# A quad's q and k loaded by 128 places, its -1 rows sent behind them, gates' inputs later, a new table of rules

## The chip, the cores and the metric

The kernel runs on one core of a Trainium2 chip, in one launch. The metric is the time of that launch on the device in microseconds (us), and lower is better. All times below come from runs of the kernel before, and from one execution of it that was profiled.

## The reference, cut to what matters

Two attention layers, A and B, work on the same input x (2048 tokens of 640 numbers), each with weights of its own, and a gate for each token mixes their outputs. A layer has 32 heads of 20 numbers, and goes through the tokens in 4 segments of 512. In a segment each head does causal softmax attention, and reads a memory M, z that the segments before have filled:

```python
for s in range(N):                                   # N = 4 segments of L = 512
    qs, ks, vs = q[:, :, s], k[:, :, s], v[:, :, s]
    logits = einsum("bhqd,bhkd->bhqk", qs, ks) * scale + mask
    a_dot = einsum("bhqk,bhkd->bhqd", softmax(logits), vs)
    a_mem = (phi(qs) @ M) / (phi(qs) @ z + 1e-6)
    outs.append(g * a_mem + (1.0 - g) * a_dot)
    M, z = M + phi(ks).T @ vs, z + phi(ks).sum()     # by head
...
g = sigmoid((x * gate_w).sum(-1, keepdims=True))
return g * layer(x, A) + (1 - g) * layer(x, B)
```

## The kernel before, in words

**Windows and quads.** The work is cut into 8 windows t: 4 segments times 2 layers. A window first makes q, k and v by products with the weights. TensorE works in a reduced f32 form, so each factor is split into a high and a low part, and a product is three products (high by high, low by high, high by low). The q and k so made (three rows for each number: the high part, the low part, and one of the two again) are written to DRAM tiles `qd[t]` and `kd[t]` and read back in another arrangement: 8 *quads* u of 4 heads each, 64 quads i = 8t + u in all.

**A quad's tiles.** `qst` and `kst` (4 buffers of each, `NQ`) are tiles of 128 places (partitions) by 2 pairs by 512 tokens. Two heads stand above each other, at places 0 and 64, and the pairs stand side by side. A head takes 3 x 20 = 60 places. The next two places of a head hold, in q, the high and low part of each row's maximum, and in k the number -1, so that a product over 62 places gives a score less its row's maximum.

**Loading a quad** (`load_quads`, L1013). Four DMAs fill a quad's tiles: q and k, each for the upper and the lower half of the places. One such DMA moves 60 places of 2 pairs of 512 numbers; its source is walked as 60 x 2 x 512, and so is its destination. The -1 rows are written once, at the start, by a memset of each whole k tile on POOL (L276), and no load touches them. A quad can be loaded when its q and k are in DRAM and the quad that had the buffer 4 quads ago is done with it (`t_over`).

**A quad's steps.** S units (`s_unit`) make scores, and DVE finds their row maxima (L1058). The maxima are turned by TensorE and sent by two small DMAs into the q tile (L1108). T units (`t_unit`) then make the transposed scores with the maxima taken off, ACT takes the exponential (L1153), and POOL cuts it at the diagonal (L1154). `pv_unit` multiplies by v (L1181), and `fin_unit` weighs and stores the result.

**What sets the order.** The kernel writes its instructions out by hand, with a small planner: a clock of its own, a queue for each of ACT, DVE, POOL and SP with a cost for each instruction, and two lanes for the two halves of TensorE's rows. A product of 128 rows is cut in two halves of 64 rows, which run beside each other. For each of the slots i (`RULES`, L90) a row of the table gives the order of S and T units and five numbers: how far the units are spread over the slot, how loaded DVE may be for side work, the lag before a unit goes on in the other half, the room that is kept, and how early the slot begins. The planner only fixes the order in which each engine gets its instructions. On the chip each engine takes its own in that order and waits where data are not there. All DMAs are issued from SP's queue, in its order; an instruction that waits there holds up all behind it. Between slots TensorE is filled with the products for this window and the next (`fill_gen`).

**The gate.** `token_gate` loads 4 tiles of x and weighs them with `gate_w`; the first 4 are asked for at job 4.

**The end.** The last window's output product is split: `job_early` does 3 of 5 blocks k of the contraction, and `job_last` (L976) the other two, after the last transposes. Each block k needs the transposed output in two parts, high (ACT) and low (DVE, from the high part). For each of 5 row tiles m, `finish` adds what was kept and sends the sum to the output.

Of the kernel before, what the change touches and what calls it, by code (L numbers as in the profile page):

```python
# [18 lines left out]
P = 128  # L19
D = 640  # L20
# [17 lines left out]
def r32(ap):  # L38
    return ap.bitcast(F32)
# [3 lines left out]
def tile_gated_mix_infini_attn(  # L43
# [44 lines left out]


    RULES = {  # L90
        0: "STSTSTSTST 1.010 2.38 0.36 8 0.0",
        1: "TSTSTSTSTS 1.010 2.19 0.30 8 0.0",
        3: "TSTSTSTSTS 1.010 2.38 0.30 8 0.0",
        4: "TSTSTSTSTS 1.010 2.38 0.32 6 0.0",
        5: "TTSSTTSSTS 1.010 2.38 0.30 8 0.0",
        6: "TSTSTSTSTS 1.010 2.38 0.30 8 0.0",
        8: "TSTSTSTSTS 1.045 2.38 0.30 4 0.0",
        9: "TSTSTSTSTS 1.010 2.38 0.35 8 0.0",
        10: "TSTSTSTSTS 1.021 2.38 0.32 8 0.0",
        12: "TSTSTSTSTS 1.010 2.38 0.30 8 0.0",  # L100
        14: "TSTSTSTSTS 0.957 2.38 0.37 6 0.0",
        15: "TSTSTSTSTS 0.932 2.30 0.32 8 0.0",
        16: "TSTSTSTSTS 1.010 2.38 0.30 8 0.0",
        19: "TSTSTSTSTS 1.002 2.63 0.30 8 0.0",
        21: "TSTSTSTSTS 1.010 2.51 0.30 4 0.0",
        22: "TSTSTSTSTS 0.927 1.90 0.30 4 0.0",
        23: "TTSTSTSTSS 1.012 2.26 0.37 8 0.0",
        24: "TSTSTSTSTS 1.010 2.38 0.30 8 0.0",
        25: "TSTSTSTSTS 1.010 3.35 0.30 8 0.0",
        27: "TSTSTSTSTS 1.010 2.38 0.30 8 0.0",  # L110
        28: "TSTSTSTSTS 0.939 3.03 0.35 8 0.0",
        30: "TSTSTSTSTS 1.010 2.38 0.30 8 0.0",
        32: "TTSTSTSTSS 1.010 2.38 0.30 8 0.0",
        34: "TSTSTSTSTS 1.010 2.38 0.30 8 0.0",
        36: "TSTSTSTSTS 1.040 2.50 0.30 6 0.0",
        37: "TSTSTSTSTS 0.950 2.38 0.30 6 0.0",
        39: "TSSTTSSTTS 1.010 1.60 0.37 8 0.0",
        41: "TSSTTSSTTS 1.010 2.38 0.33 6 0.0",
        42: "TSTSTSTSTS 0.939 2.38 0.30 4 0.0",
        46: "TSTSTSTSTS 1.010 2.38 0.30 8 0.0",  # L120
        49: "TSTSTSTSTS 1.010 2.38 0.25 4 0.0",
        50: "TSTSTSTSTS 1.010 2.38 0.30 8 0.0",
        54: "TSSTTSSTTS 1.019 3.32 0.30 6 0.0",
        57: "TSTSTSTSTS 1.010 2.38 0.30 8 0.0",
        58: "TSTSTSTSTS 1.014 3.04 0.30 8 0.0",
        60: "TSTSTSTSTS 1.010 2.38 0.30 8 0.0",
        61: "STSTSTSTST 1.047 2.95 0.38 8 6.0",
        62: "TSTSTSTSTS 1.010 2.38 0.30 8 0.0",
        63: "TSTSTSTSTS 1.014 2.38 0.25 4 0.0",
        64: "TSTSTSTSTS 1.010 2.38 0.30 8 0.0",  # L130
    }
    rule = {}
    DONE = {"A": 0.165, "D": 0.11, "G": 0.1, "S": 0.0}
# [32 lines left out]
    def put(e, dur, emit, then=None, prio=5):  # L166
        heapq.heappush(ready[e], (prio, next(seq), dur, emit, then))
        load[e] += dur
        start_next(e)

    def dma(us, emit, then=None, prio=5, lat=1.1, some=False):

        def issued():
            dma_free[0] = max(clk[0] + 0.9, dma_free[0]) + us
            if not some:
                dma_free[0] = dma_free[1] = max(dma_free[0], clk[0] + 0.9 + us, dma_free[1] + us)
            if then:
                at(dma_free[0] + lat, then)

        put("S", 0.37, emit, issued, prio)  # L180
# [88 lines left out]
    def small_tiles():  # L269
        make_identity(nc, ident)  # L270
        nc.gpsimd.memset(tri, 0.0)
        nc.gpsimd.affine_select(
            out=tri[:, L - P:], in_=tri[:, L - P:], pattern=[[-1, P]], base=0,
            channel_multiplier=1, compare_op=ALU.is_ge, fill=NEG,
        )
        for t in kst:  # L276
            nc.gpsimd.memset(r32(t), -1.0)

    def idle_step():
        z = qst[0][:, 0, :]  # L280
# [293 lines left out]

    Ot = {}
    O_store = Store([sb.tile([P, NB, D], F32, tag=f"O{i}", name=f"O{i}", bufs=1) for i in range(2)])
    OTs = {}
    pqTs = {}
    arrived = set()
    qk_done = set()  # L580
# [395 lines left out]
    def job_last(t):  # L976

        s = t // 2
        pps = {}

        def finish(m):
            if m not in kept:
                at(clk[0] + 0.3, lambda: finish(m))
                return
            put("D", 0.63, lambda: nc.vector.tensor_tensor(  # L985
                out=r32(kept[m]), in0=pps[m], in1=r32(kept[m]), op=ALU.add), lambda: dma(
                    0.7, lambda: nc.sync.dma_start(
                        out=outT[P * m:P * (m + 1), L * s:L * (s + 1)], in_=r32(kept[m])), prio=2), prio=2)

        for k in range(SOON, KT):  # L990
            yield from hold_on(lambda: (t, k) in OTs, "last")
            oh, ol = OTs[t, k]
            for m in range(KT):
                wh, wl = split[job_index[t, "early", m]]
# [3 lines left out]
                for j, (w, o) in enumerate(((wh, oh), (wl, oh), (wh, ol))):  # L998
                    yield from hold_on(lambda: not any((*firsts, *seconds, *lane_ops)), "last")
                    whole(STEP, lambda: nc.tensor.matmul(  # L1000
                        pps[m], lhsT=w[:, k, :], rhs=o, start=(k == SOON and j == 0), stop=(k == KT - 1 and j == 2)))
                    yield STEP
                if k == KT - 1:
                    after_whole(lambda m=m: finish(m))


# [1 line left out]
        t, u = divmod(i, 8)  # L1008
        return t, u, qst[i % NQ], kst[i % NQ]

    loaded, next_load, t_over = set(), [0], set()

    def load_quads():  # L1013

        while next_load[0] < 64:
            i = next_load[0]
            t, u, q, k = quad(i)
            m = (80 * u + 79) // P
            if any((t, kind, mm) not in qk_done for kind in "qk" for mm in range(m + 1)):
                return  # L1020
            if i >= NQ and i - NQ not in t_over:
                return
            next_load[0] += 1
            done = then_all(4, lambda i=i: loaded.add(i))
            r0, soon = 80 * u, marks[i - LEAD] if i >= LEAD else -2
            for dst, src in ((q, qd[t]), (k, kd[t])):
                rows = src[r0:r0 + 80, :, :].rearrange("(p f d) c n -> f (d c) p n", p=2, f=2)
                for half in range(2):
                    dma(1.0, lambda dst=dst, src=rows[half], half=half: nc.sync.dma_start(
                        out=r32(dst[64 * half:64 * half + 3 * DH, :, :]), in_=r32(src)), done, prio=soon)  # L1030

    mx, m_done, mr_done = {}, set(), set()
    t_done, p_done, s_left = {}, {}, {}
# [232 lines left out]
    def o_transpose(t, k):  # L1266
        b = bank.free.pop(0)
        px = b.rearrange("p (n c) -> p n c", c=P)

        def got(hi, lo):  # L1270
            def end():
                bank.give(b)
                OTs[t, k] = (hi, lo)

            put("A", 0.49, lambda: nc.scalar.copy(hi, b), lambda: put("D", 0.63, lambda: nc.vector.tensor_tensor(
                out=lo, in0=b, in1=r32(hi), op=ALU.subtract), end, prio=2), prio=2)
# [164 lines left out]


    warm_up()
    put("G", 6.0, small_tiles, prio=0)
    put("G", 1.6, ones_tiles, prio=1)
    for k in range(KT):
        if k < len(HEAD0):
# [89 lines left out]
```

## Time and profile before

| What | us |
|---|---|
| Time, median of 3 runs (lowest, highest) | 1039.98 (1039.63, 1041.46) |
| The profiled execution's own time | 1040.3 |
| Its span, from the first to the last instruction | 1038.6 |
| ACT busy | 661.7 |
| POOL busy | 581.7 |

The granted clock of TensorE is 0.999 over the whole span. The span lies 1.7 us below the profiled execution's own time, which is the median of the runs shown to within 0.4 us, so numbers worked out from the trace can be set against either.

The profile's page gives the busy time of each engine, the time of the DMA packets, the chain of work that ended last, the costliest groups of instructions and the DMA issues. A window's row gives, for a stretch of the span, the busy time of PE, PEld, DVE, ACT and POOL, the granted clock, the share of the time that the 16 DMA engines were busy, and GB/s.

### The profile page before, as it was taken

What the parts mean: (1) busy time and instruction counts of PE and PEld (TensorE: products, weight loads), DVE (VectorE), ACT (ScalarE), POOL (GpSimd) and SP (SyncE); (2) the same over time, 40 slices, a digit from 0 to 9 for tenths busy, and PEclk for the clock granted to TensorE, in tenths of its full rate; (3) what the DMA queues carried; (4) which work ended last, traced back from release to release, by engine and by line L of the source; (5) the groups of instructions that cost most, each with busy time, mean ns of one, the idle gap of its engine ahead of it and who ended that gap; (6) DMA issues with size and microseconds to landing.
All of it is one profiled execution on the core that took longest, in us unless ns stands there. A gap on an engine that the chain in (4) does not pass through costs nothing.

```text
span 1038.6 us, 31967 instructions
## 1 busy us (share of the span) xinstructions
PE 1031.3 (99%) x11780; PEld 874.8 (84%) x11780; DVE 765.4 (74%) x2726; ACT 661.7 (64%) x1336; POOL 581.7 (56%) x1043
## 2 busy tenths in 40 slices
PE   9999999999999999999999999999999999999998
PEld 7988888898888879898888978989879888888876
DVE  4687787579686788676886868865787867778764
ACT  6367666578565585666756567665676656657681
POOL 4465555566454564666645557555674537636471
PEclk9999999999999999999999999999999999999999
DMA  8996767478466686755855568675585865847531
GB/s 275 290 290 201 224 195 230 132 225 271 143 194 187 181 272 175 241 150 158 261 171 190 172 176 290 194 211 174 161 253 157 266 167 181 273 125 244 140 120 51
DMA packets 110028, 207.97 MB, mean 200 GB/s; under 512 B 12464, under 2 KB 16560, under 8 KB 109872
## 3 DMA queue, kind: packets, MB, share of 16 engines
q1 hardware_dynamic: 109872, 205.93, 65.7%
q8 instruction: 93, 1.52, 0.6%
q14 instruction: 63, 0.52, 0.2%
HBM read 131.43 MB, written 73.40 MB: 197 GB/s over the span
## 4 chain that ended last, share of the span: by engine, by line
PE 92%; DVE 1%; ACT 0%; issue 0%; ACTq 0%; DVEq 0%
PE bank L640 53%; PE bank L1181 14%; PE bank L1071 7%; PE bank L1161 7%; PE bank L787 4%; PE bank L749 3%; PE bank L827 3%; PE bank L1096 1%; PE bank L1000 0%; DVE row L985 0%; ACT p L1153 0%; DVE bank L1058 0%; DVE row L593 0%; ACT row L932 0%; DVE bank L592 0%
## 5 line engine op out<-in xcount | busy, mean ns | idle before, releaser
L1058 DVE CUSTOM_DVE_ANT_0 bank<-bank,tri 128x128 f32<-128x128 f32 (+3 forms) x1024 | 475.1, 518 | 157.4 <-PE bank L1071 126.0
L640 PE MATMUL bank<-row,wh 64*128 64x512 f32 x2308 | 525.7, 404 | 0.0
L1153 ACT ACTIVATE p<-bank 128x512 f32<-128x512 f32 x592 | 326.5, 599 | 141.6 <-PE bank L1161 112.8
L1154 POOL TENSOR_SCALAR_AFFINE_SELECT p<-p 128x256 f32<-128x256 f32 (+1 forms) x592 | 213.9, 369 | 268.5 <-ACT p L1153 252.1
L640 PEld LDWEIGHTS bank<-row,wh 64*128 64x128 f32 x2308 | 326.1, 185 | 11.8 <-issue 1.8
L640 PE MATMUL bank<-row,wl 64*128 64x512 f32 x1154 | 310.3, 402 | 0.0
L469 POOL TENSOR_TENSOR wl<-wst,wh 128x640 fp32r<-128x640 f32 x115 | 179.6, 1565 | 72.0 <-ACT wh L467 71.5
L640 PE MATMUL bank<-wvh,row 64*128 64x320 f32 x1280 | 189.8, 316 | 0.0
L640 PEld LDWEIGHTS bank<-row,wl 64*128 64x128 f32 x1154 | 175.0, 185 | 5.6 <-issue 0.6
L1161 PE MATMUL bank<-qst,kst 62*128 62x128 f32 (+3 forms) x1024 | 173.5, 319 | 0.0
L1071 PE MATMUL bank<-kst,qst 60*128 60x128 f32 (+3 forms) x1024 | 171.7, 320 | 0.2
L640 PEld LDWEIGHTS bank<-wvh,row 64*128 64x128 f32 x1280 | 154.1, 185 | 3.9 <-issue 2.0
L1181 PE MATMUL bank<-p,vst 128*32 128x384 f32 (+3 forms) x1932 | 146.0, 430 | 0.0
L1058 DVE DVE_READ_ACCUMULATOR2_ANT mx<- 128x1 f32 x1024 | 143.3, 140 | 0.0
L1071 PEld LDWEIGHTS bank<-kst,qst 60*128 60x128 f32 x1024 | 123.7, 185 | 12.0 <-issue 2.5
L1161 PEld LDWEIGHTS bank<-qst,kst 62*128 62x128 f32 x1024 | 124.9, 185 | 7.5 <-issue 1.2
L1181 PEld LDWEIGHTS bank<-p,vst 128*32 128x32 f32 x1932 | 58.3, 109 | 85.7 <-issue 61.4
L640 PE MATMUL bank<-wvl,row 64*128 64x320 f32 x640 | 109.4, 312 | 0.0
L467 ACT CAST wh<-wst 128x640 fp32r<-128x640 f32 x119 | 86.2, 735 | 30.8 <-PE bank L640 15.5
L640 PEld LDWEIGHTS bank<-wvl,row 64*128 64x128 f32 x640 | 85.0, 185 | 0.5 <-issue 0.2
L609 DVE TENSOR_TENSOR row<-bank,row 128x512 fp32r<-128x512 f32 x80 | 54.9, 688 | 38.3 <-ACT row L602 18.4
L1206 ACT COPY row<-bank 128x512 f32<-128x512 f32 x60 | 35.2, 587 | 70.7 <-PE bank L1181 68.8
(100 smaller groups left out, 1289.9 us busy)
## 6 DMA issues: line engine op xcount, KB each, us to landing
qd<-row SPq DMA_DIRECT2D x120, 256.0 KB
kd<-row SPq DMA_DIRECT2D x120, 256.0 KB
qst<-qd SPq DMA_DIRECT2D x128, 240.0 KB
kst<-kd SPq DMA_DIRECT2D x128, 240.0 KB
wst<-in_a_wq_dram SPq DMA_DIRECT2D x20, 320.0 KB
wst<-in_a_wk_dram SPq DMA_DIRECT2D x20, 320.0 KB
wst<-in_b_wq_dram SPq DMA_DIRECT2D x20, 320.0 KB
wst<-in_b_wk_dram SPq DMA_DIRECT2D x20, 320.0 KB
```

The lines of the kernel that those rows point to most:

```text
L467: put("A", 0.66, lambda: nc.scalar.copy(wh, w3), lambda: put(lo_eng, lo_cost, lambda: lo.tensor_tensor(out=wl, in0=w3, in1=r32(wh), op=ALU ...
L469: lambda: lo.tensor_tensor(out=wl, in0=w3, in1=r32(wh), op=ALU.subtract), end, prio=3), prio=6)
L609: put("D", 0.63, lambda: nc.vector.tensor_tensor(out=lo, in0=src, in1=r32(hi), op=ALU.subtract), out, prio=1)
L640: return nc.tensor.matmul(bank_of, lhsT=w[ROWS[half]], rhs=x_[ROWS[half]], start=start, stop=stop)
L787: return nc.tensor.transpose(px[:, n, r], block(n)[r], ident[r, r])
L1058: put("D", w / 960.0 + 0.112, lambda: nc.vector.tensor_tensor_reduce(out=sc[:, off:off + w], in0=sc[:, off:off + w], in1=tri[:, L - w:], s ...
L1071: lane_ops[half].append((w * 0.000458, lambda pair=pair, qb=qb, off=off, w=w, r=r, sc=sc: nc.tensor.matmul(sc[:, off:off + w], lhsT=q[r, p ...
L1153: put("A", 0.49, lambda: nc.scalar.activation(pt, sc, AF.Exp, scale=SCALE), lambda: (bank.give(sc), put("G", 0.08 + 0.16 * len(todo), lamb ...
L1154: "G", 0.08 + 0.16 * len(todo), lambda: nc.gpsimd.affine_select(out=blocks, in_=blocks, pattern=[[0, len(todo)], [1, P]], base=0, channel_ ...
L1161: lane_ops[half].append((w * 0.000458, lambda pair=pair, kb=kb, off=off, w=w, r=r, sc=sc: nc.tensor.matmul(sc[:, off:off + w], lhsT=k[r, p ...
L1181: nc.tensor.matmul(po[32 * j:32 * j + 32, P * kb:], lhsT=vst[t % 2][:, kb, h * E1:h * E1 + 32], rhs=pts[i, n, f][0][:, off:off + w], start ...
L1206: either(0.52, lambda: nc.scalar.copy(r32(oT), po), 0.63, lambda: nc.vector.tensor_copy(r32(oT), po), end, 2)
```

## The change

**Loads.** Of the 8 quads of a window, the first seven are loaded one pair of heads at a time: again four DMAs, q and k, each for pair 0 and pair 1. The destination is now all 128 places of one pair, 128 x 1 x 512. The source is two heads by 64 rows by 512, with the heads 60 rows apart: 4 rows more are read of each head than it has, and they fall on the 4 places behind its 60. In k they overwrite the -1 rows, so two small DMAs follow, each of 2 places from a DRAM tile `minus`, and T units wait for them (`with_ones`). In q the maxima overwrite them later, as before. The eighth quad, which would read past the end, is loaded as before. The planner counts 0.7 us for such a DMA and not 1.0.

**Start.** One k tile is set to -1 by POOL and not four; two rows of it are sent to `minus`.

**Gates.** The first four `token_gate`s are asked for at job 7 and not at job 4.

**The last product.** The high part of a transposed block is known as `OThs` as soon as ACT has it. `job_last` begins a block with high parts alone, and waits for the low part only before its first product that reads it; the first product of row tile 1 is put ahead of it. The sum and the store of the last row tile go in two halves of 256 columns.

**Table.** `RULES` has 43 rows in place of 40, with other orders and numbers.

```diff
     RULES = {
-        0: "STSTSTSTST 1.010 2.38 0.36 8 0.0",
+        0: "TSTSTSTSTS 1.010 2.12 0.30 8 0.0",
...
-        for t in kst:
-            nc.gpsimd.memset(r32(t), -1.0)
+        nc.gpsimd.memset(r32(kst[3]), -1.0)
...
+    minus = dram.tile([2, 2, L], F32R, name="minus")
...
+            n = 2 if m == KT - 1 else 1
+            for a in range(n):
+                c = slice(L // n * a, L // n * (a + 1))
+                put("D", 0.63 / n, lambda c=c: nc.vector.tensor_tensor(
+                    out=r32(kept[m])[:, c], in0=pps[m][:, c], in1=r32(kept[m])[:, c], op=ALU.add), lambda c=c: dma(
+                        0.7 / n, lambda: nc.sync.dma_start(
+                            out=outT[P * m:P * (m + 1), L * s + c.start:L * s + c.stop], in_=r32(kept[m])[:, c]), prio=2), prio=2)
+
+        def steps(k):
+
+            for m in range(KT):
+                for j in range(3):
+                    if not (m == 1 and j == 0 or m == 0 and j == 2):
+                        yield m, j
+                    elif m == 0:
+                        yield 1, 0
+                        yield 0, 2
...
-            yield from hold_on(lambda: (t, k) in OTs, "last")
+            yield from hold_on(lambda: (t, k) in OThs, "last")
...
+                if j == 2:
+                    yield from hold_on(lambda: (t, k) in OTs, "last")
...
-            done = then_all(4, lambda i=i: loaded.add(i))
-            r0, soon = 80 * u, marks[i - LEAD] if i >= LEAD else -2
-            for dst, src in ((q, qd[t]), (k, kd[t])):
-                rows = src[r0:r0 + 80, :, :].rearrange("(p f d) c n -> f (d c) p n", p=2, f=2)
-                for half in range(2):
-                    dma(1.0, lambda dst=dst, src=rows[half], half=half: nc.sync.dma_start(
-                        out=r32(dst[64 * half:64 * half + 3 * DH, :, :]), in_=r32(src)), done, prio=soon)
+            r0, soon = 80 * u, marks[i - LEAD] if i >= LEAD else -2
+            if u == 7:
...
+                continue
             done = then_all(4, lambda i=i: loaded.add(i))
+
+            def ones(i=i, k=k):
+                got = then_all(2, lambda: with_ones.add(i))
+                for half in range(2):
+                    r = 64 * half + 3 * DH
+                    dma(0.3, lambda r=r: nc.sync.dma_start(out=r32(k[r:r + 2, :, :]), in_=r32(minus)), got, prio=soon, some=True)
+
+            k_there = then_all(2, ones)
+            for dst, src, then in ((q, qd[t], done), (k, kd[t], lambda done=done, k_there=k_there: (done(), k_there()))):
+                rows = src[r0:r0 + 80, :, :].rearrange("d c n -> (d c) n")
+                for p in range(2):
+                    heads = bass.AP(tensor=rows.tensor, offset=rows.offset + 6 * DH * L * p, ap=[[3 * DH * L, 2], [L, 64], [1, L]])
+                    dma(0.7, lambda dst=dst, heads=heads, p=p: nc.sync.dma_start(
+                        out=r32(dst[:, p, :]), in_=r32(heads)), then, prio=soon)
...
-            if i == 4:
+            if i == 7:
                 for n in range(NB):
                     token_gate(n)
...
-        return lambda: i in loaded and i in mr_done and p_room()
+        return lambda: i in loaded and i in with_ones and i in mr_done and p_room()
```

**How instructions move: SP's queue in window 0.** These are SP's DMAs at the place where quads 1 and 2 are loaded, in the order in which SP takes them, first of the kernel before. `wst` are weights and x, `mr` a quad's row maxima, and the sizes are those of the destination.

```order
L536 DMA wst_125<-in_x_dram 128x640
L1029 DMA qst_81<-qd_97 60x2x512 x2
L1029 DMA kst_85<-kd_105 60x2x512 x2
L1029 DMA qst_82<-qd_97 60x2x512 x2
L1029 DMA kst_86<-kd_105 60x2x512 x2
L1108 DMA qst_80<-mr_147 2x8x128 x2
L475 DMA wst_126<-in_a_wk_dram 128x640
L451 DMA wst_125<-in_a_wv_dram 128x640
```

The same place of SP's queue in the kernel after:

```order
L1065 DMA qst_81<-qd_97 128x1x512 x2
L1065 DMA kst_85<-kd_105 128x1x512 x2
L1065 DMA qst_82<-qd_97 128x1x512 x2
L1065 DMA kst_86<-kd_105 128x1x512 x2
L478 DMA wst_126<-in_a_wk_dram 128x640
L454 DMA wst_127<-in_a_wv_dram 128x640
L1057 DMA kst_85<-minus 2x1024
L1144 DMA qst_80<-mr_148 2x8x128 x2
L1057 DMA kst_85<-minus 2x1024
L1057 DMA kst_86<-minus 2x1024 x2
```

The loads stay together. New are the DMAs of the -1 rows (L1057). The first of them waits until the two loads of that quad's k have landed, and it now stands ahead of quad 0's row maxima, which were sent right behind the loads.

**TensorE at the last product.** These are the last transposes (`ident`, `O`) and the first products of block k = 3 in `job_last`, of the kernel before. The first name is the bank that is written, and a row tile m has a bank; `row_18924` is the high part and `row_18925` the low part.

```order
L1000 MATMUL bank_122<-row_18924_17134,wh_130 128x512
L787 MATMUL bank_124<-ident,O_144 128x64 x8
L1000 MATMUL bank_122<-row_18924_17134,wl_131 128x512
L1000 MATMUL bank_122<-row_18925_17135,wh_130 128x512
L1000 MATMUL bank_123<-row_18924_17134,wh_132 128x512
L1000 MATMUL bank_123<-row_18924_17134,wl_133 128x512
L1000 MATMUL bank_123<-row_18925_17135,wh_132 128x512
```

The same place in the kernel after, where `row_19265` is the high part and `row_19266` the low part:

```order
L790 MATMUL bank_120<-ident,O_145 128x64 x8
L1017 MATMUL bank_119<-row_19265_17216,wh_135 128x512
L1017 MATMUL bank_119<-row_19265_17216,wl_136 128x512
L1017 MATMUL bank_125<-row_19265_17216,wh_131 128x512
L1017 MATMUL bank_119<-row_19266_17217,wh_135 128x512
L1017 MATMUL bank_125<-row_19265_17216,wl_132 128x512
L1017 MATMUL bank_125<-row_19266_17217,wh_131 128x512
```

Three products with the high part now stand ahead of the first with the low part, where two stood before, and the transposes stand ahead of the whole block.

More of the change, by code (lines that the diff above doesn't have):

```diff
@@ L113, in tile_gated_mix_infini_attn @@
[L113 to L123, printed above, removed]
@@ L984, in finish @@
                 return
[L985 to L988, printed above, removed]
+            n = 2 if m == KT - 1 else 1
[13 more added lines that the diff above has]
+                        yield 0, 2
         for k in range(SOON, KT):
-            yield from hold_on(lambda: (t, k) in OTs, "last")
-            oh, ol = OTs[t, k]
-            for m in range(KT):
-                wh, wl = split[job_index[t, "early", m]]
+            yield from hold_on(lambda: (t, k) in OThs, "last")
+            for m, j in steps(k):
                 if m not in pps:
@@ L997, in job_last @@
                     pps[m] = bank.free.pop(0)
[L998 to L1003, printed above, removed]
+                if j == 2:
+                    yield from hold_on(lambda: (t, k) in OTs, "last")
+                yield from hold_on(lambda: not any((*firsts, *seconds, *lane_ops)), "last")
+                (wh, wl), (oh, ol) = split[job_index[t, "early", m]], OThs[t, k]
+                whole(STEP, lambda: nc.tensor.matmul(
+                    pps[m], lhsT=(wl if j == 1 else wh)[:, k, :], rhs=ol if j == 2 else oh,
+                    start=(k == SOON and j == 0), stop=(k == KT - 1 and j == 2)))
+                yield STEP
+                if k == KT - 1 and j == 2:
                     after_whole(lambda m=m: finish(m))
@@ L1273, in end, with low @@
                 OTs[t, k] = (hi, lo)
-            put("A", 0.49, lambda: nc.scalar.copy(hi, b), lambda: put("D", 0.63, lambda: nc.vector.tensor_tensor(
-                out=lo, in0=b, in1=r32(hi), op=ALU.subtract), end, prio=2), prio=2)
+            def low():
+                OThs[t, k] = (hi, lo)
+                put("D", 0.63, lambda: nc.vector.tensor_tensor(
+                    out=lo, in0=b, in1=r32(hi), op=ALU.subtract), end, prio=2)
+            put("A", 0.49, lambda: nc.scalar.copy(hi, b), low, prio=2)
         def turned():
@@ L1443, in tile_gated_mix_infini_attn @@
     warm_up()
-    put("G", 6.0, small_tiles, prio=0)
+    put("G", 3.0, small_tiles, lambda: dma(0.3, lambda: nc.sync.dma_start(
+        out=r32(minus), in_=r32(kst[3][:2, :, :])), prio=17, some=True), prio=0)
     put("G", 1.6, ones_tiles, prio=1)
```

75 lines of the change are left out of this document (47 added, 28 removed).

## The prediction

> **What bounds the kernel now.** I read the page first (busy times, DMA packets, chain), then TensorE's waits, then windows and single lines for the parts that change.
>
> ```profile
> span 1038.6 us, 31967 instructions
> PE 1031.3 (99%) x11780; PEld 874.8 (84%) x11780; DVE 765.4 (74%) x2726; ACT 661.7 (64%) x1336; POOL 581.7 (56%) x1043
> DMA packets 110028, 207.97 MB, mean 200 GB/s; under 512 B 12464, under 2 KB 16560, under 8 KB 109872
> q1 hardware_dynamic: 109872, 205.93, 65.7%
> PE 92%; DVE 1%; ACT 0%; issue 0%; ACTq 0%; DVEq 0%
> ```
>
> TensorE sets the end: 92% of the chain that ended last is its own. SP's queue (q1) fills 65.7% of 16 DMA engines' span, so transfers have room, but not twofold.
>
> ```profile
> PE bank L281 <- DVE qst L285: 1.5, 1, 1.5
> PE bank L1096 <- ACT p L1153: 0.7, 1, 0.7
> ```
>
> These two are all that TensorE's matmuls are shown to wait for (us in total, times, longest). No quad load is among them: faster loads have almost nothing to remove, slower ones can become the bound.
>
> **The loads: on how many DMA engines does one run?** This decides the time. The rows of the DMA list, first and last with those between left out, give 891 issues:
>
> ```profile
> qd<-row SPq DMA_DIRECT2D x120, 256.0 KB
> ...
> qst<-qd SPq DMA_DIRECT2D x128, 240.0 KB
> kst<-kd SPq DMA_DIRECT2D x128, 240.0 KB
> ...
> qst<-mr SPq DMA_DIRECT2D x128, 8.0 KB
> ...
> beta<-in_a_beta_dram SPq DMA_DIRECT2D x1, 16.0 KB
> beta<-in_b_beta_dram SPq DMA_DIRECT2D x1, 16.0 KB
> ```
>
> 256 are quad loads (outermost count 60 on both sides), 128 are row maxima (16 source rows, 2 destination places), 507 walk 128 rows on both sides. The page counts 12464 packets under 512 B. The two `beta` DMAs make 256 of them (128 rows of 128 B each); I read the other 12208 as one end mark for each engine that a DMA ran on. All on 16 engines would be 14256. With 16 engines for the 507, 15 for the 256 and 2 for the 128 it is 8112 + 3840 + 256 = 12208, to the packet. 15 is the largest number up to 16 that divides 60, and 2 the largest that divides 16 and 2. So **the outermost counts of source and destination limit the spread**.
>
> The Trainium skill says this outright ("DMA: Bandwidth & Descriptors", section "Why a DMA increments its semaphore by 16 and not by 1"): a DMA uses the largest number of engines up to 16 that divides the outermost count of both access patterns, and the hardware-queued ones take the lowest-numbered engines; the count agrees with its first half, and no row names the engines. By this rule the sum is the forecast below.
>
> The new load's destination is 128 places, but its source is 2 heads by 64 rows by 512, and the heads lie 60 rows apart, so the two counts can't be joined. If the 2 counts, a load runs on **two** engines, engine 0 say with head 0, and the other 14 carry none of it.
>
> Are they always the same two? Window rows (columns as on any such row: stretch, busy times, clock, DMA share, GB/s):
>
> ```profile
> 978.50:982.75 4.25, 4.25 (x42) 2.49 (x43) 2.81 (x8) 3.09 (x7) 3.04 (x8) 1.00 0.99 252
> 1035.00:1036.25 1.25, 0.00 (x0) 0.00 (x0) 0.00 (x0) 0.00 (x0) 0.00 (x0) 0.96 1.06 374
> ```
>
> The first is four quad loads back to back, the second the output's stores, which are 128 rows. The share runs a little over 1 where all 16 are full; 0.99/1.06 is 0.93, near 15/16. With 15 engines for each load, one engine stayed idle through all four, so I take it that the set does not change.
>
> **The price of a load.** Before: 245,760 B at 252 GB/s are 0.98 us. After: 262,144 B, half on each of two engines. An engine moves 374/16 = 23.4 GB/s in the store row, and 252/15 = 16.8 GB/s in the load row. So a load takes 131,072/23.4k = 5.6 us, at most 7.8 us. In the load row 15 engines write to 60 places at once; two engines writing to places far apart are nearer to the store row, so I take 5.6. No row shows two engines alone, which may be up to a tenth faster; I keep that as the low end.
>
> Work on each of the two engines (estimates from these rows):
> - new loads, 56 quads x 4 = 224 by 5.6: **1254** (1747 at 7.8);
> - the rest of the traffic: 0.657 x 1038.6 = 682 us for each engine, less the old loads' 256 x 0.98 = 251, is 431; at the store row's rate the same 144.5 MB/16 would take 386. I take **415**;
> - the eighth quads, still 32 loads of 0.98: **31**; the 112 DMAs of -1 rows, 4 KB on each engine at 23.4 GB/s: **20**.
>
> That is 1720 us on two engines, against 1031 on TensorE: the bound moves to these two. To it comes time when they have no quad to load:
>
> ```profile
> 0.00:20.00 20.00, 18.48 (x96) 14.07 (x98) 9.46 (x17) 12.15 (x22) 9.77 (x21) 1.00 0.80 271
> 978.00:1038.60 60.60, 55.31 (x544) 41.13 (x540) 31.90 (x104) 32.52 (x66) 26.73 (x54) 0.98 0.32 100
> ```
>
> Loads are issued from 19.8 to 978.6 us (SP's rows, further down). Outside, the engines were busy 0.80 x 20 = 16 and 0.32 x 60.6 = 19 us of 80.6, which the sum has; **45** are added.
>
> **The new wait on SP.** The DMA of the -1 rows waits for its k to land, and SP's queue stands behind it: the next loads, weights, x, stores and row maxima. In window 0 quad 0's maxima stand behind quad 1's k, 22 us of load.
>
> ```profile
> 977.26 0.79 SPq L1029 DMA_DIRECT2D qst<-qd  x2
> ...
> 977.25:978.25 1.00, 1.00 (x12) 0.98 (x10) 1.00 (x7) 1.00 (x3) 0.31 (x1) 1.00 0.16 8
> 1036.75:1038.60 1.85, 0.00 (x0) 0.00 (x0) 0.00 (x0) 0.00 (x0) 0.00 (x0) 0.50 0.02 6
> ```
>
> Two loads were issued at 977.26, and in the next 1.0 us next to nothing moved. So each time that SP stands until the engines are dry, they lose some 1 us at the start. The last row bounds the word that data have landed: the last store's packets are through at 1036.75, and the span ends 1.85 us later. From 0 (something else is still queued) to 2.85 us by 56 quads; I take 1.5: **84**.
>
> Sum: 1720 + 45 + 84 = 1849, forecast **1850 us**. Does TensorE keep up? A quad costs the two engines 22.4 + 7.4 = 30 us, TensorE 1031/64 = 16. Between the end of a quad's T units and the S units of the quad that takes its buffer the planned order has one slot: two periods have to hold one load and one slot's work, 30 + 16 = 46 < 60. So the engines stay the bound and TensorE waits at S units.
>
> **What the other edits are worth.** SP issues a load in 0.4 us:
>
> ```profile
> L1029 SPq DMA_DIRECT2D qst<-qd x128: 315/372/1296, 19.8 to 977.7; - x128
> L1029 SPq DMA_DIRECT2D kst<-kd x128: 316/411/1623, 20.7 to 978.6; - x128
> L1108 SPq DMA_DIRECT2D qst<-mr x128: 610/617/1039, 38.9 to 1005.6; - x128
> L277 POOL MEMSET kst<- x4: 952/952/953, 2.1 to 4.8; 128x1024 f32 x4
> L527 DVE CUSTOM_DVE_ANT_0 wst<-wst,gw x16: 812/819/1670, 36.8 to 661.9; 128x640 f32<-128x640 f32 x16
> ...
> SPq L1029 <- PE bank L1161: 109.1, 38, 8.2
> SPq L1108 <- ACT p L1153: 71.0, 23, 7.4
> SPq L622 <- ACT row L625: 52.4, 32, 5.1
> ```
>
> The maxima's DMA, whose sides differ in shape as the new load's do, takes 0.62. 224 by 0 to 0.2, and 112 new issues by 0.3 to 0.4, are 34 to 90 us on SP, whose three longest waits alone are 232 us: nothing. Three memsets fewer (2.9 us of POOL, 56% busy): nothing. The gates' four tiles later: they move 1.3 MB within window 0, by 0 either way.
>
> The table moves units within slots. TensorE idles 1038.6 - 1031.3 = 7.3 us in all; I let the table win or lose half of that, -4 to +4, in the old regime, and 0 where DMA is the bound.
>
> The end:
>
> ```profile
> 1027.84 0.69 DVE L1275 TENSOR_TENSOR row<-bank,row 128x512 fp32r<-128x512 f32 x1 [0.84 <-ACT row L1275]
> 1031.36 3.44 DVE L985 TENSOR_TENSOR row<-bank,row 128x512 f32<-128x512 f32 x5 [2.83 <-PE bank L1000]
> ```
>
> The last add (0.69) in halves lets its store begin 0.35 earlier, less one more issue; beginning a block before its low part hides up to 0.69. Together 0 to -1 us: -0.7.
>
> **Rivals.**
> - **B, faster: the destination alone decides.** The row maxima's 2 is also the count of their destination, so the packets don't exclude it. Then a load runs on 16 engines, 262,144 B at 374 GB/s in 0.70 us, the engines win some 70 us of work each that nothing waits for, and 1040 - 0.7 - 2 of the table gives **1037**. It decides if 128 places are cut in 16 while the source is cut in 2 by 64. For: a limit is only seen here with the smaller count on the destination. Against: an engine would have to start amid a head of the source. Another rule of the Trainium skill speaks for B (same page, "Rules for kernel authors": rather than two transfers to disjoint halves of the places, use one over 128); by it the time is that of B.
> - **C, two engines, but other ones each time.** Four loads run side by side in some 6 us, not 4; TensorE waits nowhere, since one slot lies between: **1040**. Against it: the 0.93.
> - **D, 16 engines, and the -1 rows bind.** T units wait for a DMA after the load; 1 us of TensorE at each of 56 quads: **1095**. For it only SP's order speaks.
>
> **How the numbers follow.** Two engines, the same ones: 0.82, forecast 1850. B 0.12, C 0.03, D 0.03. The bounds of the first: low, a rate a tenth higher (1254 and 415 fall by 152) and no dry time (84): 1613; high, 7.8 us a load: 2343, of which I take 2250, since its row has 15 engines writing at once. The range 1600 to 2250 holds all but some 2 in 100 of the first case, so 0.80. Under 0.2% is what a measurement of this kernel can't tell from no change. Faster: two thirds of B, 0.08. Same: the rest of B and half of C, 0.06. Slower: 0.86.
>
> **What would show it.** Right: PE far under 99%, PE or PEld waiting for DMA `qst<-qd` and `kst<-kd` at S units; loads of 5 us and more; packets under 512 B at 12464 - 224 x 13 + 113 x 2 + 16 = 9794 if each load leaves 2 marks (12930 if 16; the 113 are the DMAs of -1 rows, the 16 the added store); GB/s down to some 115. Wrong: 12930 packets and PE at 99%. If marks are 2 and the time is still near 1040, C holds, and the engines are not fixed.

## The result and the profile after

| | before | after |
|---|---|---|
| Time, median (lowest, highest), us | 1040.1 (1039.63, 1041.46) | 1973.46 (1971.59, 1975.79) |
| The profiled execution's span, us | 1038.6 | 1974.1 |
| Granted clock of TensorE over the span | 0.999 | 0.777 |

The ratio of the medians is 1.897, with a 95% interval of 1.894 to 1.900. The forecast was 1850, in a range of 1600 to 2250: the direction and the mechanism held, the size came out 6.7% above.

The page of the kernel after, its first rows: busy time of each engine, the tenths of granted clock in 40 slices, the packets, SP's queue, and the chain that ended last by engine. L1065 is the new load, L1107 an S unit, L1197 a T unit, L643 a product.

```profile
span 1974.1 us, 32002 instructions
PE 1192.7 (60%) x11780; PEld 1008.4 (51%) x11780; DVE 768.9 (39%) x2723; ACT 664.7 (34%) x1340; POOL 581.0 (29%) x1040
...
PEclk8787777788766987778886688767797687876879
...
DMA packets 109504, 212.56 MB, mean 108 GB/s; under 512 B 9794, under 2 KB 14146, under 8 KB 109348
...
q1 hardware_dynamic: 109348, 210.52, 31.5%
...
DMA 28%; PE 19%; SPq 9%; issue 1%; DVE 1%; ACT 1%; POOL 0%; DVEq 0%; ACTq 0%
```

Three rows carry it. The packets under 512 B are 9794, the number that the prediction gave for two marks a load; 16 marks would be 12930. Less the 256 of the `beta` DMAs, all of them are packets of 4 B on SP's queue, 9538 here and 12208 before: these are the marks. The bytes rose by 2% and the rate fell from 200 to 108 GB/s. TensorE's share of the chain fell from 92% to 19%; DMAs and SP's queue stand there now. The chain could be followed back only to 784 us, over 60% of the span (93% before), so TensorE holds about a third of what was followed. The work of DVE, ACT and POOL is the same within 0.5%, and their share has halved: the engines wait.

What TensorE waits for, the longest three rows of its waits (us in total, times, longest), where before there were 2.2 us in all:

```profile
PE bank L1197 <- DMA qst<-mr: 127.7, 12, 24.5
PE bank L1107 <- DMA kst<-kd: 114.7, 19, 11.8
PE bank L1107 <- ACT p L1189: 100.1, 9, 25.0
```

The k loads stand in front of the S units, as the prediction said. The first row it did not name. T units wait up to 24.5 us for row maxima, 8 KB in a DMA. Its destination has two places, so by the prediction's own count it too runs on two engines, and it stands behind the loads there. That chain of causes is read from the row and that count; no run took the maxima alone away from the loads. In experiment 5, which moves the loads to another queue and leaves the maxima in SP's, this wait is 20.7 us.

One quad's loads are to be seen on SP's timeline (start, us, line, transfer, how many), with the window rows of the same stretch behind it (stretch, busy PE, PEld, DVE, ACT, POOL, granted clock, DMA share, GB/s):

```profile
1005.87 1.14 SPq L1065 DMA_DIRECT2D qst<-qd  x2
1007.06 8.73 SPq L1065 DMA_DIRECT2D kst<-kd  x2
1029.78 0.54 SPq L1057 DMA_DIRECT2D kst<-minus  x2
```

```profile
1008.00:1018.00 10.00, 10.00 (x151) 9.96 (x150) 8.20 (x31) 5.75 (x12) 3.47 (x6) 1.00 0.14 51
1045.00:1057.00 12.00, 0.00 (x0) 0.00 (x0) 0.00 (x0) 0.00 (x0) 0.00 (x0) 0.50 0.22 73
```

With four loads under way the share is 0.14 and the rate 51 GB/s. SP's queue has the following part of it in these 10 us (packets, MB, share of 16 engines); the rest is two packets of another queue, with instructions.

```profile
q1 hardware_dynamic: 236, 0.48, 12.8%
```

Two engines of 16 are 12.5%, and 48 GB/s are 24 for each, a little over the 23.4 of an engine in the store row of before. The trace's packets show the loads end one after another: their marks stand in pairs at 1013.3 and 1013.4, 1018.5 and 1018.7, 1023.8 and 1024.0, 1029.0 and 1029.2 us, so a load takes 5.3 us. From the first issue to the -1 rows' DMA, which waits for k, 23.9 us pass, of which the four loads are 21. In the second window row a weight and the loads of another quad are under way, and for 12 us no compute engine does anything.

### The profile page after: what moved, and what is told of

Same layout as the page of the kernel before. It is cut to its first block, busy times and chain, and to the rows that moved or that the text cites. A ratio compares the mean times of both kernels' runs of the same rounds, so it can differ in the third digit from the quotient of the medians.

```text
span 1974.1 us, 32002 instructions
## 1 busy us (share of the span) xinstructions
PE 1192.7 (60%) x11780; PEld 1008.4 (51%) x11780; DVE 768.9 (39%) x2723; ACT 664.7 (34%) x1340; POOL 581.0 (29%) x1040
## 2 busy tenths in 40 slices
DMA packets 109504, 212.56 MB, mean 108 GB/s; under 512 B 9794, under 2 KB 14146, under 8 KB 109348
## 4 chain that ended last, share of the span: by engine, by line
DMA 28%; PE 19%; SPq 9%; issue 1%; DVE 1%; ACT 1%; POOL 0%; DVEq 0%; ACTq 0%
DMA kst<-kd 15%; PE bank L643 11%; SPq L1065 7%; PE bank L1217 2%; DMA wst<-in_a_wv_dram 2%; PE bank L1197 2%; DMA wst<-in_b_wv_dram 2%; DMA row<-in_xT_dram 2%; PE bank L1107 2%; DMA wst<-in_a_wq_dram 2%; DMA qst<-mr 2%; PE bank L790 1%; SPq L1144 1%; DMA wst<-in_x_dram 1%; DMA wst<-in_a_wk_dram 1%
## 5 line engine op out<-in xcount | busy, mean ns | idle before, releaser
L1094 DVE CUSTOM_DVE_ANT_0 bank<-bank,tri 128x256 f32<-128x256 f32 (+3 forms) x1024 | 477.3, 518 | 713.9 <-PE bank L1107 640.9
L643 PE MATMUL bank<-row,wh 64*128 64x512 f32 x2308 | 599.1, 446 | 39.8 <-ACT p L1189 27.2
L1107 PE MATMUL bank<-kst,qst 60*128 60x128 f32 (+3 forms) x1024 | 201.5, 363 | 339.2 <-DMA kst<-kd 114.7
L643 PEld LDWEIGHTS bank<-row,wh 64*128 64x128 f32 x2308 | 376.7, 211 | 52.5 <-ACT p L1189 27.6
L1197 PE MATMUL bank<-qst,kst 62*128 62x512 f32 (+3 forms) x1024 | 200.8, 355 | 288.5 <-DMA qst<-mr 127.7
L643 PE MATMUL bank<-row,wl 64*128 64x512 f32 x1154 | 343.5, 440 | 0.0
L1107 PEld LDWEIGHTS bank<-kst,qst 60*128 60x128 f32 x1024 | 145.9, 216 | 360.0 <-issue 122.5
L1197 PEld LDWEIGHTS bank<-qst,kst 62*128 62x128 f32 x1024 | 148.1, 209 | 304.5 <-issue 158.2
L643 PE MATMUL bank<-wvh,row 64*128 64x320 f32 x1280 | 222.6, 345 | 0.0
L643 PEld LDWEIGHTS bank<-row,wl 64*128 64x128 f32 x1154 | 200.7, 211 | 5.9 <-issue 1.4
L643 PEld LDWEIGHTS bank<-wvh,row 64*128 64x128 f32 x1280 | 182.9, 211 | 1.8 <-issue 0.8
L447 POOL TENSOR_TENSOR wvl<-wst,wvh 128x640 fp32r<-128x640 f32 (+1 forms) x48 | 63.8, 1330 | 242.7 <-ACT wvh L444 229.8
L643 PE MATMUL bank<-wvl,row 64*128 64x320 f32 x640 | 127.7, 343 | 0.0
L790 PE MATMUL bank<-ident,row 64*128 64x64 f32 x752 | 89.5, 248 | 34.3 <-ACT p L1189 34.1
L444 ACT CAST wvh<-wst 128x640 fp32r<-128x640 f32 (+1 forms) x48 | 30.5, 642 | 224.8 <-DMA wst<-in_a_wv_dram 131.8
```

Of the source, the lines that this page charges most:

```text
L447: put("G", 0.8 * n, lambda: nc.gpsimd.tensor_tensor(out=wl[:, a:b, :], in0=w3, in1=r32(wh[:, a:b, :]), op=ALU.subtract), end, prio=4)
L643: return nc.tensor.matmul(bank_of, lhsT=w[ROWS[half]], rhs=x_[ROWS[half]], start=start, stop=stop)
L790: return nc.tensor.transpose(px[:, n, r], block(n)[r], ident[r, r])
L1094: put("D", w / 960.0 + 0.112, lambda: nc.vector.tensor_tensor_reduce(out=sc[:, off:off + w], in0=sc[:, off:off + w], in1=tri[:, L - w:], s ...
L1107: lane_ops[half].append((w * 0.000458, lambda pair=pair, qb=qb, off=off, w=w, r=r, sc=sc: nc.tensor.matmul(sc[:, off:off + w], lhsT=q[r, p ...
L1197: lane_ops[half].append((w * 0.000458, lambda pair=pair, kb=kb, off=off, w=w, r=r, sc=sc: nc.tensor.matmul(sc[:, off:off + w], lhsT=k[r, p ...
```

## Experiments

Each kernel is compared with the kernel before, run on the same chip (1040.3 to 1041.1 us). A time without an interval is a single execution, which differences of hundreds of us can stand on.

**1. The loads and -1 rows alone,** put into the kernel before, with its own table, its gates and its last product:

```diff
-                rows = src[r0:r0 + 80, :, :].rearrange("(p f d) c n -> f (d c) p n", p=2, f=2)
...
+                    heads = bass.AP(tensor=rows.tensor, offset=rows.offset + 6 * DH * L * p, ap=[[3 * DH * L, 2], [L, 64], [1, L]])
...
```

> The kernel before with the new loads, their -1 rows and the shorter memset, and nothing else of the change (old table, gates and last product). Two engines carry the loads: 1900 to 2050 us, with 9778 packets under 512 B (9794 less the 16 marks of the store that is not cut in two). If the table or the order at the end made the time, it stays near 1040 us.

One execution: 1972.42 us, with 9778 packets under 512 B. These edits alone give the whole loss; the other three change nothing next to it.

**2. The same bytes on 16 engines.** Each load takes one half of the places and both pairs, so that both sides are walked as 64 x 2 x 512. Bytes, rows and -1 DMAs stay.

```diff
-                for p in range(2):
-                    heads = bass.AP(tensor=rows.tensor, offset=rows.offset + 6 * DH * L * p, ap=[[3 * DH * L, 2], [L, 64], [1, L]])
...
-                        out=r32(dst[:, p, :]), in_=r32(heads)), then, prio=soon)
+                for f in range(2):
+                    heads = bass.AP(tensor=rows.tensor, offset=rows.offset + 3 * DH * L * f, ap=[[L, 64], [6 * DH * L, 2], [1, L]])
...
+                        out=r32(dst[64 * f:64 * f + 64, :, :]), in_=r32(heads)), then, prio=soon)
```

First with 1.0 us a load in the planner, as the old loads had:

> The kernel after with the same rows and bytes loaded (64 rows of a head, 256 KB a load, -1 rows sent behind and waited for), but each load takes one half of the places and both pairs, so that source and destination are both walked as 64 x 2 x 512. Two engines theory, by outermost counts: 16 engines, 12930 packets under 512 B, 1034 to 1050 us. If the -1 rows' wait on SP's queue or the 4 extra rows make the time, it stays above 1300 us.

1068.61 us, 1.0265 (1.0242 to 1.0288): 19 us above the upper end of what was expected. Then with the 0.7 of the change, so that every engine's instructions stand in the order of the kernel after:

> As the run of loads in halves of 64 places, but the planner is given the change's own 0.7 us for a load, so that every engine gets its instructions in the very order of the kernel after; only the shape of a load differs (64 x 2 x 512 on both sides, 16 engines by the counts). If two engines a load are the whole loss: 1030 to 1050 us, with 12930 packets under 512 B. If the change's order or its -1 rows carry a part of the loss, above 1060.

1068.33 us, 1.028 (1.0255 to 1.0306). Its page, SP's issues of the loads (ns, shortest/median/longest), and a window with all four loads in it:

```profile
DMA packets 112640, 212.57 MB, mean 199 GB/s; under 512 B 12930, under 2 KB 17282, under 8 KB 112484
...
PE 82%; DMA 9%; ACT 3%; POOL 2%; DVE 2%; issue 2%; SPq 1%; ACTq 0%; DVEq 0%; POOLq 0%
```

```profile
L1065 SPq DMA_DIRECT2D kst<-kd x112: 573/599/2200, 22.9 to 998.6; - x112
```

```profile
997.50:1003.50 6.00, 6.00 (x70) 3.82 (x66) 4.37 (x19) 3.49 (x10) 1.65 (x6) 1.00 0.86 229
```

Of the waits, SP's for k and TensorE's for k:

```profile
SPq L1057 <- DMA kst<-kd: 132.7, 87, 5.7
...
PE bank L1107 <- DMA kst<-kd: 3.0, 4, 1.7
```

12930 packets under 512 B: 16 engines for each load. SP still waits for k before each -1 DMA, 132.7 us in all, and TensorE hardly notices. Same order, same bytes, same -1 rows and their wait, and 905 us less. So two engines cost **905 us of the 933**. The 28 us that are left belong to something else, which the sixth group looks for.

**3. Half the dose: q alone, or k alone, on two engines.** This asks whether SP's wait for k, with its -1 DMA, keeps the engines dry. The other tile is loaded by halves as before, at 0.7 in the planner. With q alone on two engines there are no -1 DMAs at all. The diff is that with q alone; with k alone the condition reads `dst is k`.

```diff
+                if dst is q:
...
+                else:
+                    rows = src[r0:r0 + 80, :, :].rearrange("(p f d) c n -> f (d c) p n", p=2, f=2)
...
```

> The kernel after with q loaded by 128 places (112 loads on two engines) and k as before, without any DMA of -1 rows. The two engines have 112 x 5.4 = 605 us of loads, 144 old ones of 0.98 (141) and the rest's 415: 1161, and some dry time: 1150 to 1350 us. If the wait for -1 rows is most of the loss, below 1100; if one load on two engines in a quad delays as much as four loads do, near 1970.

> The kernel after with k loaded by 128 places (112 loads on two engines, and the DMAs of -1 rows that wait for them) and q as before: the counterpart of the run with q so loaded, which took 1455 us without any DMA of -1 rows. The two engines carry the same work but for 20 us. If SP's wait for k to land is what keeps them dry, 56 x 2 us and more longer: above 1550. If the dry time has other causes: within 3%, 1410 to 1500.

One execution each: 1454.54 with q, 1468.76 with k. SP's own waits with k:

```profile
SPq L1058 <- DMA kst<-kd: 438.0, 54, 14.5
```

SP stands for 438 us in that row, a row that the kernel with q alone doesn't have, and the two times are within 1%. The first time lies 105 us above the upper end of what was expected, the second in the band for dry time of other causes. With q alone SP waits for loads elsewhere, but less: over all its instructions its waits for DMAs are 295 us, against 481 with k. So the -1 wait is **not needed** for a loss of this size; what it costs with both tiles on two engines, no run shows by itself. Nor is the slow issue needed. In the kernel after, an issue of a k load takes 4 us at the median; with k alone it is short again:

```profile
L1065 SPq DMA_DIRECT2D qst<-qd x112: 485/528/5147, 20.1 to 1884.7; - x112
L1065 SPq DMA_DIRECT2D kst<-kd x112: 493/3986/8067, 21.4 to 1886.9; - x112
```

```profile
L1067 SPq DMA_DIRECT2D kst<-kd x112: 490/521/6850, 21.2 to 1387.8; - x112
```

The price of a load is not constant: from 0 loads (1068) to 112 it is 3.4 to 3.6 us a load, from 112 to 224 it is 4.5 to 4.6.

**4. The order.** The planner counts 0.7 us for a load that takes 5.4. One number is changed:

```diff
-                    dma(0.7, lambda dst=dst, heads=heads, p=p: nc.sync.dma_start(
+                    dma(5.4, lambda dst=dst, heads=heads, p=p: nc.sync.dma_start(
```

> The kernel after, with one number changed: the planner counts 5.4 us on SP's queue for each of the 224 new loads, and not 0.7, so that TensorE, SP and the others get their work in an order made for slow loads. The two engines' own work stays some 1690 us (224 x 5.4 and the rest). Theory one: the two engines run dry for some 285 us since the order was made for loads of 0.7 us, and what is queued behind and between them comes at wrong places; then 1700 to 1880. Theory two: they run dry since a load can't go before the quad 4 places earlier is done with the buffer, and the quad's own chain of load, maxima and T units has to follow, whatever the order: 1920 to 2050. A planner that puts 22 us on SP's queue for each quad may also push weights and maxima late, and give more than 2050.

One execution: 1831.56 us, with the same 9794 packets. Theory one holds for 142 us: an order made for fast loads is part of the loss. The waits of SP show the change: the wait for k has fallen from 458.5 us to this, and SP now stands before the maxima:

```profile
SPq L1144 <- ACT mr L1149: 138.3, 24, 18.8
SPq L1144 <- ACT p L1189: 137.6, 24, 13.7
SPq L625 <- ACT row L628: 118.4, 26, 13.1
SPq L1057 <- DMA kst<-kd: 108.6, 32, 7.2
```

A count of the packets in the traces, the time of each span by how many packets of SP's queue are in flight:

```
                 none   1 or 2   3 and more   span
before            248       57          734   1039
q alone           213      501          739   1452
k alone           198      553          716   1467
order for 5.4     130     1054          646   1830
after             217     1129          629   1974
```

The marks are left out of this count. "1 or 2" is the time when hardly anything but loads moves. Against after, the new order takes 87 us from "none" and 75 from "1 or 2", and adds 17 to "3 and more".

**5. Another queue.** The 224 loads, in the same shape, are issued from POOL.

```diff
-                    dma(0.7, lambda dst=dst, heads=heads, p=p: nc.sync.dma_start(
+                    dma(0.7, lambda dst=dst, heads=heads, p=p: nc.gpsimd.dma_start(
```

> The kernel after with the 224 loads of 128 places issued from POOL's queue in place of SP's; all else as in the kernel after. If such a load runs on the same two engines whichever queue issues it: 1800 to 2000 us. If POOL's queue spreads it over more engines, or takes others each time: 1060 to 1200.

One execution: 1297.14 us, between the two expectations, with POOL busy 753.0 us where it was 581.0. The queue's row and the time from issue to landing:

```profile
q0 software_dynamic: 118272, 59.54, 18.6%
```

```profile
DMA to landing us min/median/max: 8.1/10.7/14.7
```

In the trace's packets on this queue, 14336 are of 4096 B (161 ns at the median) and 3584 of 4 B, the marks, 16 for each load. The other 100,352 are of 8 B, and no run shows what they are for. More than two of the 4096 B packets are under way at once in most of the time that there are any. A load by itself isn't fast: 8.1 us at best. But loads run beside each other, and SP's DMAs are in another queue. The time is 676 us shorter than with SP's queue. SP waits for k as long as ever, but none of the 224 loads stands behind it any more, so this run doesn't price that wait. The T units' wait for the row maxima has fallen from 127.7 us to the second row:

```profile
SPq L1057 <- DMA kst<-kd: 534.2, 56, 19.4
PE bank L1197 <- DMA qst<-mr: 20.7, 5, 6.8
```

It looks like what rival C supposed (two engines, other ones each time), though not at C's 1040 us, and with POOL's own work on top. What the other engines and what the other queue gave was not separated. The Trainium skill ("DMA: Bandwidth & Descriptors", section "Why a DMA increments its semaphore by 16 and not by 1") says that a copy issued from GpSimd marks on all 16 engines and, where it runs on fewer, takes neighbours from a cursor that goes round: 3584 = 224 x 16 agrees, and for which engines carried the data the trace has no row.

**6. The other 28 us.** First everything of the change but its loads: the kernel after, with all quads loaded in the old way.

```diff
-            if u == 7:
+            if True:
```

> The kernel after with all quads loaded as before (60 places, no -1 rows sent, all four k tiles set at the start), so table, gates and last product alone. Two engines theory: 1034 to 1044 us. If the table is what slows it, near 1970.

1078.34 us, 1.0365 (1.0351 to 1.0379): a miss, 38 us slower with loads like those before. Then the table alone, in the kernel before:

```diff
     RULES = {
-        0: "STSTSTSTST 1.010 2.38 0.36 8 0.0",
+        0: "TSTSTSTSTS 1.010 2.12 0.30 8 0.0",
...
```

> The kernel before with the new table alone. The run with the new table and the old loads took 1078 us. If the table is what costs there (it was made for other plans), 1060 to 1090; if gates or the last product cost, near 1040.

1071.44 us, 1.0301 (1.028 to 1.0322). And the reverse, gates and last product with the old table and old loads. The `minus` tile, the DMA that fills it and the planner's cost for the start (3.0 us and not 6.0) stay as in the change:

> The kernel before with the gates' later request and the new last product (old loads, old table). If the table is what costs in the run with old loads: 1036 to 1046. If these two edits cost: 1060 to 1090.

1067.24 us, 1.0258 (1.0244 to 1.0272). Each of the two runs lies in the band that said that its own edits cost. So the table costs, and so does the rest *without* the table. Since the last product alone costs nothing (experiment 7), these 27 us come with the gates' later request or with the start; no run parts the two. What table and rest share is that the planner makes another plan. The page hardly shows it. Table alone, the first row of the page and the longest of TensorE's waits:

```profile
PE 1056.5 (99%) x11780; PEld 893.0 (84%) x11780; DVE 762.8 (72%) x2724; ACT 664.0 (62%) x1338; POOL 584.2 (55%) x1043
```

```profile
PE bank L284 <- DVE qst L288: 1.5, 1, 1.5
PE bank L643 <- ACT mr L1116: 0.9, 1, 0.9
```

PE is busy 99% as before, with 1056.5 us in place of 1031.3 for the same 11780 instructions. TensorE works in two halves of 64 rows; while one half waits and the other works, PE counts as busy. The table below gives, for each half, the time between the starts of its matmuls beyond what the first of the two takes, and halves the sum, since a gap idles one half of the rows. It is an estimate, since the trace doesn't name the half of a product:

```
                        gaps over 0.3 us    their sum, halved, us
before                                78                     18.9
table alone                          159                     45.9
gates and last product               144                     43.3
old loads                            152                     49.3
64 x 2 x 512, 0.7                    120                     42.7
```

24 to 30 us more in each, against 27 to 38 us in time. The sizes hang on how products are put to halves. With products put to the two in turn, the sums are 8 us for before and 19 to 34 for the four others; with each put to the half that came free last before it, 38 and 58 to 68. By every count the plan of before has fewer such gaps than each of these four. That these gaps are all of the loss is not shown. Why just these gaps appear, slot by slot, was not traced.

**7. The last product alone,** in the order of before up to the end:

```diff
-            yield from hold_on(lambda: (t, k) in OTs, "last")
+            yield from hold_on(lambda: (t, k) in OThs, "last")
...
+            n = 2 if m == KT - 1 else 1
```

> The kernel before with the new last product alone (high parts first, the last sum and store in halves); all other instructions stand in the order of before. By the working: 0 to -1 us, so 1039 to 1040.5, same. If this edit costs something on the path: above 1042.

1040.61 against 1040.32 us, 1.0004 (0.9996 to 1.0013): the same. None of the kernels run beats the kernel before.

## Why the prediction was right, and where its sum was off

- **The spread of a load over engines: right, to the packet.** 9794 for two engines, and 12930 for 16 when both sides begin with 64. The smaller count stood on the source alone, which before's trace could not show, and that closes rival B. The rule of the Trainium skill that the prediction weighed (same page and section as above: the largest number up to 16 that divides both outermost counts) agrees. The rule of the Trainium skill that spoke for B (same page, "Rules for kernel authors": one transfer over 128 places rather than two halves) is measured against here: two halves were 905 us faster, since the one transfer over 128 places has a source that begins with 2.
- **Always the same two engines: right.** Four loads queued together move at 48 GB/s, and one ends after another, 5.3 us apart, and the time followed. On POOL's queue, where it seems not to hold, the time was 676 us shorter.
- **The price of a load: 5.6 forecast; 5.3 (between the marks) to 5.4 us measured** (64 packets of 2 KB on an engine, 84 ns each at the median in the trace's packets). The bound of 7.8 was far off. At 5.4 the term of the loads is 1210, not 1254.
- **The time with no load to carry: mis-sized, and this is the step that failed.** The prediction had 45 + 84 = 129 us. The loads at 5.4 and its other terms (415 + 31 + 20) are 1676, so 1974 leaves **some 298**. For 217 of these no packet of SP's queue is in flight (the table of experiment 4), which is dry time for certain. The other 81 are the two engines idle beside others, or other traffic that took more than the 466 given to it; the trace doesn't name a packet's engine. And the prediction laid 84 of its 129 on SP's wait for the -1 rows, by 56 quads. Experiment 3 speaks against that place: with half of the loads on two engines, the time with and without that wait was within 1%. What holds instead, for 142 us, is that the instructions stand in an order made for loads of 0.7 us (experiment 4), and 87 of these are less time with nothing in flight. That what the order puts between and ahead of loads comes late, and so lets the engines run dry, is argued from this. The other some 160 us stay open. SP's stalled issues and the turn of a quad's four buffers are candidates; no run separated them. The ends of windows are not where quads lie far apart: from window 1 on, SP issues quads 25 to 43 us apart inside a window, 30 at the median, and 20 to 26 us apart where a window ends.
- **"So the engines stay the bound": half right.** Two engines are the longest resource, but no packet of SP's queue is in flight for 217 us, and in the part of the chain that could be followed DMA, PE and SP's queue take turns (28, 19 and 9% of the span). The comparison of two periods (46 against 60 us) took the engines for always fed.
- **SP's issue of a load at 0.4 to 0.6 us: right at the median for the first two loads of a quad (0.53), wrong for the next two (4.0).** The prediction held it for nothing; what it cost is not separated.
- **The table at -4 to +4: far too narrow.** It is +31 us alone (1071.44 - 1040.54). The step took TensorE's idle 7.3 us for all that an order can win or lose. By the count of experiment 6 the order also decides how often one half waits while the other works, which the page counts as busy. It didn't matter next to 905 us; it would have turned rival B from 1037 into some 1068, slower and not faster.
- **Rival D, the -1 rows: not seen.** With loads on 16 engines and the -1 rows kept, the time (1068) is that of the new plans without such rows (1067 to 1078), not 1095.
- **The last product at -0.7: not to be told from nothing.**
- **The gates and the start at 0: not so with the old loads.** The run of gates and last product is 27 us slower than before, and the last product has no part in it. Next to 905 us it didn't matter.

## What to carry to other kernels

Before widening a DMA to all 128 places, look at the outermost count of *both* sides: a source of 2 blocks ran on 2 of 16 engines here and cost 905 us, and the same bytes walked as 64 x 2 x 512 on both sides did not. On SP's queue the count of the 4 B packets told the number of engines of a DMA exactly, before and after, and it is the first thing to check when a rate halves. On POOL's queue it did not: 16 for each load, whatever carried it. Where a planner sets the order, every edit to costs or tables is a new plan, and a busy share of 99% is no bound on what it can lose when an engine works in halves.

## What the runs showed of the hardware

- SP's issue is not free when few engines are behind it: with two loads of 262,144 B queued on two engines the next ones took 4.0 us at the median and 8.1 at most to issue, where the same instruction took 0.5 with the engines free (0.52 at the median with k alone on two engines).
- TensorE's granted clock fell with its idle time: 0.50 in the 12 us in which no compute engine worked, 1.00 in a busy stretch some 30 us earlier, and 0.777 over the span. A 64 x 512 product (L643) took 446 ns on average where it took 404 before, so the busy time of TensorE grew too, for the same instructions:

```profile
L643 PE MATMUL bank<-row,wh 64*128 64x512 f32 x2308 | 599.1, 446 | 39.8 <-ACT p L1189 27.2
```

- A DMA engine alone with one other moved 24 to 24.7 GB/s (48 GB/s on two, and 262,144 B on two in 5.3 us), against 23.4 with all 16 at work (the store row of before).
